# Attention scores and values as 64x64 matmuls on quarters of the array, in a kernel of chunked attention and two expert layers

## The chip, the cores and the metric

The kernel runs on one core of a Trainium2 chip. Its time is the device time of one execution in microseconds; the kernel before takes 1247.1 us (median of three runs, 1245.94 to 1248.13). A core has five engines that work through their own instruction queues and wait for one another with semaphores: PE (TensorE, matmuls out of SBUF into PSUM), DVE (VectorE), ACT (ScalarE), POOL (GpSimd) and SP, which here only issues DMAs. PSUM has eight banks of 128 partitions x 512 f32.

## The reference, cut to what matters

```python
# attention in chunks of 64 tokens; q, k, v are (4, 8, 576, 64)
scores = (q_c @ k_c.T) / sqrt(64)            # 64 x 64 for each batch, head and chunk
scores = scores - max(scores, axis=-1)
attn = exp(scores); attn = attn / (sum(attn) + 1e-9)
x = (attn @ v_c) -> (2304 tokens, 512)
# four relu experts with given shares
out = sum_e p[:, e] * (relu(x @ w1[e]) @ w2[e])    # 512 -> 1024 -> 512
# a gated layer
y = (silu(out @ w_gate) * (out @ w_val)) @ w_out   # 512 -> 1536 -> 512
```

## The kernel before, in words

The 2304 tokens are 18 blocks of 128 tokens. A block holds two chunks of 64 tokens (c = 0, 1) and 8 heads, which lie as 4 pairs (i) of two heads (h). Attention of block a runs in four stages on PE, each followed by work of DVE and ACT:

- **scores** (att_scores, L255): 8 matmuls, one for each pair and chunk. Queries and keys lie with two heads on the 128 partitions (64 each). The keys are laid out with zero blocks (kbd), so that one matmul over 128 rows and 64 columns of the array, with 128 columns streamed, gives both heads. All goes into one PSUM tile of 128 x 512. DVE then takes the maximum (L276) and subtracts it (L277, att_soft), and ACT takes the exponential (L283, att_exp).
- **transposes** (att_turn, L294): four 128x128 transposes through PE into PSUM, a copy of ACT to SBUF (et, L298), and the sums and reciprocals on DVE (att_sums, L302).
- **values** (att_values, L317): 8 matmuls as in the scores, with the values and their zero blocks (vbd); DVE multiplies the result by the reciprocals (L330).
- **output transposes** (att_out, L336): four transposes and a copy of ACT (for blocks 6 to 17: xb, L357), then a DMA.

The zero blocks are written once, by memsets of DVE and POOL at the start (L812), before any matmul of attention.

Blocks 0 to 5 run first (L869 to L918), with the first plain products of the expert layer (plain, L652) behind them. Their stages take PSUM tiles in turn from three pools of two banks each: psA, psX and psY. Blocks 6 to 17 are spread over the expert layer: the list `rest` (L953) holds their 48 stages in order, and they are taken from it one at a time, four in the beginning (`ahead`, L989) and the others in the main loop (L1088):

```python
if rest and now[0] % NPROD < 5:
    stage, a = rest.pop(0)
    stage(a, (psA, "a"))
```

The main loop goes through products: a product (L628) is six matmuls of 128x384 (L624 to L626), and seven products make a set. After four products and after the next three, PE does a piece of the second layer (y, L673 to L677). In the loop a set's products stand as 4, 5 of one set and 0, 1 of the next, y work, 6, then 2, 3, and y work again. Five of the seven are followed by one attention stage: products 6, 2, 3, 4 and 1. Between 6 and 2 and between 2 and 3 only one product stands between two stages; between 3 and 4, 4 and 1, and 1 and 6 there is more.

All stages of blocks 6 to 17 take their PSUM tile from psA, which has two banks, in turn: a stage can start when the stage that had the bank before it has been read out. After each product DVE and ACT do what belongs to it (done, L554), and behind products 6 and 4 DVE also computes two sums of weights (w_sums, L396, `raw<-raw`) before the stage's own work. Engine queues keep the order of the program.

The names in the rows: s, et, av and xt are the PSUM tiles of scores, transposes, values and output transposes; lx, lz, lw and plz, plw, plx the banks of products; hh and hl the hidden values; w the split weights; u and p copies of a product's bank.

Of the kernel before, what the change touches and what calls it, by code (L numbers as in the profile page):

```python
# [19 lines left out]
P = 128  # L20
B, H, S, D = 4, 8, 576, 64
CH = 64
# [69 lines left out]
def attention_moe_gated(  # L92
# [138 lines left out]
    def att_load(a):  # L231
        pool, how = (first_p, dict(tag="q23")) if a in (2, 3) else (at_p, dict(tag="q"))
        q = pool.tile([P, NPAIR, P], F32, name=f"q{a}", bufs=2, **how)
        if a >= 2:
            (nc.scalar if a < 4 else nc.sync).dma_start(q, qt[a])
        for h in range(2):
            b = slice(64 * h, 64 * h + 64)
            queue = nc.scalar if a < 2 and h == 0 else nc.sync
            if a < 2:
                queue.dma_start(flat(q[b]), flat(qt[a, b]))  # L240
            queue.dma_start(flat(kbd[place(a)][b, h]), flat(kt[a, b]))
        att[a] = {"q": q, "k": kbd[place(a)]}

    def att_load_v(a):
        v = vbd[place(a)]
        for h in range(2):
            b = slice(64 * h, 64 * h + 64)
            (nc.scalar if a < 2 and h == 0 else nc.sync).dma_start(flat(v[b, h]), flat(vt[a, b]))
        att[a]["v"] = v
# [4 lines left out]

    def att_scores(a, where):  # L255
        s = att[a]
        ps = att_ps(f"s{a}", where)
        for i in range(NPAIR):
            for c in range(2):
                b = slice(64 * c, 64 * c + 64)  # L260
                nc.tensor.matmul(
                    ps[b, 2 * i : 2 * i + 2], s["q"][:, i, b], s["k"][:, :, i, c], start=True, stop=True
                )
# [6 lines left out]
    def att_soft(a):  # L270
# [3 lines left out]
        pool, how = (acc_p, dict(tag="acc")) if a < BLOCKS else (at_p, dict(tag="e", bufs=3))  # L274
        e = s["e"] = pool.tile([P, H, CH], F32, name=f"e{a}", **how)
        nc.vector.tensor_reduce(out=mx, in_=ps, op=ALU.max, axis=AX.X)  # L276
        nc.vector.tensor_tensor(out=e, in0=ps, in1=mx.unsqueeze(2).to_broadcast(ps.shape), op=ALU.subtract)  # L277
# [16 lines left out]
    def att_turn(a, where):  # L294
        s = att[a]
        ps = transpose(att_ps(f"et{a}", where), s["e"])
        et = s["et"] = at_p.tile([P, H, CH], F32, tag="et", name=f"et{a}", bufs=1)
# [19 lines left out]
    def att_values(a, where):  # L317
        s = att[a]
        ps = att_ps(f"av{a}", where)
        for i in range(NPAIR):  # L320
            for c in range(2):

                nc.tensor.matmul(
                    ps[64 * c : 64 * c + 64, 2 * i : 2 * i + 2],
                    s["et"][:, 2 * i + c, :], s["v"][:, :, i, c], start=True, stop=True,
                )
# [3 lines left out]
        nc.vector.tensor_tensor(  # L330
# [845 lines left out]
```

## Time and profile before

| | |
|---|---|
| three runs, median | 1247.1 us (1245.94 to 1248.13) |
| the profiled execution | 1245.16 us, span 1243.3 us |
| PE busy | 1226.5 us (99%), 7216 matmul records |
| DVE busy | 794.0 us (64%) |
| ACT / POOL busy | 538.7 us (43%) / 595.3 us (48%) |
| DMA | 82.6% of 16 engines, 289 GB/s |

The span is the time from the first to the last instruction of the profiled execution; some 1.9 us lie around it. A matmul with f32 operands shows as two records, one with fp32r operands as one. The busy time of PE counts a matmul's whole passage, so that neighbours overlap; what a matmul costs in a dense stream is the time from its start to the start of the next.

### The profile page before, as it was taken

How to read it: one execution, taken by the hardware profiler on the slowest of the kernel's cores; microseconds unless marked ns; L12 is line 12 of the kernel's file. 1: busy time of each engine (PE TensorE's matmuls, PEld its weight loads, DVE VectorE, ACT ScalarE, POOL GpSimd, SP SyncE). 2: the span in 40 equal slices, each digit the busy share in tenths (PEclk: the TensorE clock that was granted, in tenths of full speed). 3: DMA queues.
4: the chain of work that ended last, by engine and by line, in shares of the span. 5: the costliest groups of instructions: out<-in, count | busy, mean ns of one | idle time of the engine just before them, and what ended most of it. 6: DMA issues, size and time to landing. Idle time of an engine off the chain costs nothing.

```text
span 1243.3 us, 21100 instructions
## 1 busy us (share of the span) xinstructions
PE 1226.5 (99%) x7216; PEld 1131.5 (91%) x7216; DVE 794.0 (64%) x1352; ACT 538.7 (43%) x1192; POOL 595.3 (48%) x611
## 2 busy tenths in 40 slices
PE   7999999999999999999999999999999999999998
PEld 6888888899888999898889889999999999999998
DVE  6766666666636766765566666455667656685576
ACT  4554434345424454544354344334435344344331
POOL 5553434477517776846376867312333222233221
PEclk9999999999999999999999999999999999999999
DMA  9588886799797999897899999866888797788774
GB/s 224 168 273 281 277 271 222 252 323 337 277 354 263 361 325 352 310 380 277 285 368 331 347 395 311 290 226 233 292 322 296 262 312 261 250 312 295 277 234 153
DMA packets 179594, 359.94 MB, mean 289 GB/s; under 512 B 19216, under 2 KB 46352, under 8 KB 179488
## 3 DMA queue, kind: packets, MB, share of 16 engines
q1 hardware_dynamic: 178688, 357.25, 82.6%
q10 hardware_dynamic: 768, 1.31, 0.4%
q8 instruction: 58, 0.95, 0.3%
q14 instruction: 48, 0.39, 0.1%
q0 software_dynamic: 32, 0.04, 0.0%
HBM read 258.90 MB, written 99.61 MB: 288 GB/s over the span
## 4 chain that ended last, share of the span: by engine, by line
PE 81%; DMA 7%; DVE 3%; issue 3%; POOL 2%; ACT 2%; SPq 1%; POOLq 0%; DVEq 0%; ACTq 0%
PE y L673 9%; PE y L677 9%; PE y L675 9%; PE lx L624 8%; PE lx L626 7%; PE lx L625 7%; PE ox L739 5%; PE lz L624 4%; PE oz L739 4%; PE lz L626 4%; PE lz L625 4%; DMA w<-w 3%; PE lw L624 2%; PE lw L626 2%; PE lw L625 2%
## 5 line engine op out<-in xcount | busy, mean ns | idle before, releaser
L673 PE MATMUL y<-w,hh 128*128 128x512 f32 x576 | 228.1, 396 | 0.0
L677 PE MATMUL y<-w,hl 128*128 128x512 f32 x576 | 226.4, 393 | 0.0
L675 PE MATMUL y<-w,hh 128*128 128x512 f32 x576 | 225.6, 392 | 0.2 <-POOL w L126 0.2
L126 POOL TENSOR_TENSOR w<-raw,w 128x256 fp32r<-128x256 f32 (+1 forms) x156 | 143.5, 938 | 149.7 <-ACT w L125 131.9
L126 POOL TENSOR_TENSOR ol<-sg,oh 128x384 fp32r<-128x384 f32 x72 | 80.5, 1129 | 267.1 <-ACT oh L125 225.7
L559 ACT ACTIVATE hh<-sum_p 128x384 fp32r<-128x384 f32 x90 | 47.2, 525 | 221.0 <-DVE sum_p L612 221.0
L762 DVE SCALAR_TENSOR_TENSOR acc<-y,prob,acc 128x512 f32<-128x512 f32 x126 | 91.1, 743 | 65.3 <-PE y L677 65.1
L677 PEld LDWEIGHTS y<-w,hl 128*128 128x128 f32 x576 | 108.0, 188 | 24.1
L673 PEld LDWEIGHTS y<-w,hh 128*128 128x128 f32 x576 | 108.2, 188 | 21.4 <-issue 1.4
L675 PEld LDWEIGHTS y<-w,hh 128*128 128x128 f32 x576 | 108.2, 188 | 21.3 <-POOL w L126 0.7
L612 DVE TENSOR_TENSOR sum_p<-lx,p 128x384 f32<-128x384 f32 x81 | 44.9, 554 | 94.7 <-PE lx L626 93.4
L560 DVE SCALAR_TENSOR_TENSOR hl<-sum_p,hh 128x384 fp32r<-128x384 f32 x90 | 63.0, 700 | 62.4 <-ACT hh L559 62.4
L126 POOL TENSOR_TENSOR w_made<-raw,w_made 128x256 fp32r<-128x256 f32 x84 | 68.3, 822 | 66.3 <-ACT w_made L125 54.3
L125 ACT ACTIVATE w<-raw 128x256 fp32r<-128x256 f32 (+1 forms) x156 | 67.5, 454 | 5.4 <-DVE raw L396 3.2
L125 ACT ACTIVATE oh<-sg 128x384 fp32r<-128x384 f32 x72 | 36.5, 525 | 70.4 <-DVE sg L573 70.0
L608 ACT COPY u<-lx 128x384 f32<-128x384 f32 x81 | 38.6, 477 | 65.0 <-PE lx L626 64.9
L624 PE MATMUL lz<-t1h,w 128*128 128x384 f32 x162 | 55.3, 341 | 1.7 <-DMA w<-w 1.7
L624 PE MATMUL lz<-b22h,w 128*128 128x384 f32 x162 | 55.8, 344 | 1.1 <-ACT p L608 0.9
L624 PE MATMUL lw<-b21h,w 128*128 128x384 f32 x162 | 54.8, 339 | 0.7 <-DMA w<-w 0.7
L125 ACT ACTIVATE o<-sg 128x384 fp32r<-128x384 f32 x54 | 26.5, 520 | 66.8 <-DVE sg L129 66.8
L624 PE MATMUL lx<-t2h,w 128*128 128x384 f32 x162 | 55.0, 340 | 0.3 <-DMA w<-w 0.3
L626 PE MATMUL lx<-t3h,w 128*128 128x384 f32 x162 | 54.9, 339 | 0.0
(270 smaller groups left out, 3421.0 us busy)
## 6 DMA issues: line engine op xcount, KB each, us to landing
w<-w SPq DMA_DIRECT2D x567, 256.0 KB, 5.3
w<-w SPq DMA_DIRECT2D x96, 512.0 KB, 6.0
w<-w_made SPq DMA_DIRECT2D x84, 256.0 KB, 5.7
wo_t<-wo_t SPq DMA_DIRECT2D x36, 512.0 KB, 4.8
wo_b<-wo_b SPq DMA_DIRECT2D x27, 512.0 KB, 4.2
raw<-w SPq DMA_DIRECT2D x19, 512.0 KB, 4.3
raw<-w SPq DMA_DIRECT2D x32, 256.0 KB, 4.3
sums<-x SPq DMA_DIRECT2D x40, 192.0 KB, 5.4
```

The costliest lines, as they stand in the source:

```text
L125: nc.scalar.activation(h, src, AF.Copy)
L126: (lo or nc.vector).tensor_tensor(out=l, in0=src, in1=h.bitcast(F32), op=ALU.subtract)
L559: nc.scalar.activation(h, src, AF.Relu)
L560: nc.vector.scalar_tensor_tensor(out=l, in0=src, scalar=0.0, in1=h.bitcast(F32), op0=ALU.max, op1=ALU.subtract)
L624: nc.tensor.matmul(ps, w[:, 0, c], xh[:, k], start=f, stop=False, skip_group_check=True)
L625: nc.tensor.matmul(ps, w[:, 0, c], xl[:, k], start=False, stop=False, skip_group_check=True)
L626: nc.tensor.matmul(ps, w[:, 1, c], xh[:, k], start=False, stop=e, skip_group_check=True)
L673: nc.tensor.matmul(y, hh[:, c], w[:, 0], start=(j == 0), stop=False)
L675: nc.tensor.matmul(y, hh[:, c], w[:, 1], start=False, stop=False)
L677: nc.tensor.matmul(y, hl[:, c], w[:, 0], start=False, stop=(j == 3))
L739: nc.tensor.matmul(o, left[:, c], w[:, k, right], start=start and t % 2 == 0 and k == 0 and i == 0, stop=k == 1 and i == 2, skip_group_che ...
L762: nc.vector.scalar_tensor_tensor(out=sum_, in0=y, scalar=p, in1=sum_, op0=ALU.mult, op1=ALU.add)
```

## The change

The keys and values lose their zero blocks, and with them the memsets at the start. Each block's scores and values are now 16 matmuls of 64 rows by 64 columns of the array, with 64 columns streamed: one for each pair, head and chunk. The two heads use different rows of the array and write to two PSUM tiles, which lie in two banks, so a stage of scores or values now takes both banks of its pool. DVE reads the two tiles one after the other, with operations of 128x256 in place of 128x512. In blocks 6 to 17 a block's values come two blocks behind the scores and its output transposes three (two before), and the transposes stand ahead of the values. There are two more buffers (et 2, e 4), one DMA for keys and values where there were two (blocks 2 to 17), and one pair of weight splits of the first plain product (w_plain) stands ahead of block 4's softmax.

```diff
@@ -231,36 +231,53 @@
     def att_load(a):
         pool, how = (first_p, dict(tag="q23")) if a in (2, 3) else (at_p, dict(tag="q"))
         q = pool.tile([P, NPAIR, P], F32, name=f"q{a}", bufs=2, **how)
-        if a >= 2:
-            (nc.scalar if a < 4 else nc.sync).dma_start(q, qt[a])
-        for h in range(2):
-            b = slice(64 * h, 64 * h + 64)
-            queue = nc.scalar if a < 2 and h == 0 else nc.sync
-            if a < 2:
+        k = att_tile("k", a)
+        if a < 2:
+            for h in range(2):
+                b = slice(64 * h, 64 * h + 64)
+                queue = nc.scalar if h == 0 else nc.sync
                 queue.dma_start(flat(q[b]), flat(qt[a, b]))
-            queue.dma_start(flat(kbd[place(a)][b, h]), flat(kt[a, b]))
-        att[a] = {"q": q, "k": kbd[place(a)]}
+                queue.dma_start(flat(k[b]), flat(kt[a, b]))
+        else:
+            (nc.scalar if a < 4 else nc.sync).dma_start(flat(q), flat(qt[a]))
+            nc.sync.dma_start(flat(k), flat(kt[a]))
+        att[a] = {"q": q, "k": k}
 
     def att_load_v(a):
-        v = vbd[place(a)]
-        for h in range(2):
-            b = slice(64 * h, 64 * h + 64)
-            (nc.scalar if a < 2 and h == 0 else nc.sync).dma_start(flat(v[b, h]), flat(vt[a, b]))
-        att[a]["v"] = v
+        v = att[a]["v"] = att_tile("v", a)
+        if a < 2:
+            for h in range(2):
+                b = slice(64 * h, 64 * h + 64)
+                (nc.scalar if h == 0 else nc.sync).dma_start(flat(v[b]), flat(vt[a, b]))
+        else:
+            nc.sync.dma_start(flat(v), flat(vt[a]))
+
+    def att_tile(what, a):
+        pool, tag = (first_p, what + "23") if a in (2, 3) else (at_p, what)
+        return pool.tile([P, NPAIR, 2, CH], F32, tag=tag, name=f"{what}{a}", bufs=2)
 
     def att_ps(name, where):
         pool, tag = where
         return pool.tile([P, H, CH], F32, tag=tag, name=name)
 
+    def att_halves(name, where):
+        pool, tag = where
+        return [pool.tile([P, NPAIR, CH], F32, tag=tag, name=f"{name}_{h}") for h in range(2)]
+
+    def by_head(t, h):
+        return t.rearrange("p (i h) k -> p i h k", h=2)[:, :, h]
+
+    def of_head(t, h):
+        return t.rearrange("p (i h) -> p i h", h=2)[:, :, h]
+
     def att_scores(a, where):
         s = att[a]
-        ps = att_ps(f"s{a}", where)
+        ps = att_halves(f"s{a}", where)
         for i in range(NPAIR):
-            for c in range(2):
-                b = slice(64 * c, 64 * c + 64)
-                nc.tensor.matmul(
-                    ps[b, 2 * i : 2 * i + 2], s["q"][:, i, b], s["k"][:, :, i, c], start=True, stop=True
-                )
+            for h in range(2):
+                for c in range(2):
+                    b, r = slice(64 * c, 64 * c + 64), slice(64 * h, 64 * h + 64)
+                    nc.tensor.matmul(ps[h][b, i], s["q"][r, i, b], s["k"][r, i, c], start=True, stop=True)
         if next_in_place(a) is not None:
             att_load(next_in_place(a))
         s["s"] = ps
@@ -271,10 +288,13 @@
         s = att[a]
         ps = s.pop("s")
         mx = st_p.tile([P, H], F32, tag="mx", name=f"mx{a}")
-        pool, how = (acc_p, dict(tag="acc")) if a < BLOCKS else (at_p, dict(tag="e", bufs=3))
+        pool, how = (acc_p, dict(tag="acc")) if a < BLOCKS else (at_p, dict(tag="e", bufs=4))
         e = s["e"] = pool.tile([P, H, CH], F32, name=f"e{a}", **how)
-        nc.vector.tensor_reduce(out=mx, in_=ps, op=ALU.max, axis=AX.X)
-        nc.vector.tensor_tensor(out=e, in0=ps, in1=mx.unsqueeze(2).to_broadcast(ps.shape), op=ALU.subtract)
+        for h in range(2):
+            nc.vector.tensor_reduce(out=of_head(mx, h), in_=ps[h], op=ALU.max, axis=AX.X)
+            nc.vector.tensor_tensor(
+                out=by_head(e, h), in0=ps[h], in1=of_head(mx, h).unsqueeze(2).to_broadcast(ps[h].shape), op=ALU.subtract
+            )
         if a >= BLOCKS:
             att_exp(a)
 
@@ -294,7 +314,7 @@
     def att_turn(a, where):
         s = att[a]
         ps = transpose(att_ps(f"et{a}", where), s["e"])
-        et = s["et"] = at_p.tile([P, H, CH], F32, tag="et", name=f"et{a}", bufs=1)
+        et = s["et"] = at_p.tile([P, H, CH], F32, tag="et", name=f"et{a}", bufs=2)
         nc.scalar.copy(et, ps)
         if a >= BLOCKS:
             att_sums(a)
@@ -316,20 +336,20 @@
 
     def att_values(a, where):
         s = att[a]
-        ps = att_ps(f"av{a}", where)
+        ps = att_halves(f"av{a}", where)
         for i in range(NPAIR):
-            for c in range(2):
-
-                nc.tensor.matmul(
-                    ps[64 * c : 64 * c + 64, 2 * i : 2 * i + 2],
-                    s["et"][:, 2 * i + c, :], s["v"][:, :, i, c], start=True, stop=True,
-                )
+            for h in range(2):
+                for c in range(2):
+                    b, r = slice(64 * c, 64 * c + 64), slice(64 * h, 64 * h + 64)
+                    nc.tensor.matmul(ps[h][b, i], s["et"][r, 2 * i + c], s["v"][r, i, c], start=True, stop=True)
         if next_in_place(a) is not None:
             att_load_v(next_in_place(a))
 
-        nc.vector.tensor_tensor(
-            out=s["e"], in0=ps, in1=s["rs"].unsqueeze(2).to_broadcast(ps.shape), op=ALU.mult
-        )
+        for h in range(2):
+            nc.vector.tensor_tensor(
+                out=by_head(s["e"], h), in0=ps[h],
+                in1=of_head(s["rs"], h).unsqueeze(2).to_broadcast(ps[h].shape), op=ALU.mult,
+            )
 
     x_first = {}
 
@@ -794,31 +814,11 @@
         st_p = at_cm.enter_context(tc.tile_pool(name="st", bufs=3, side="right"))
         first_cm = ExitStack()
         first_p = first_cm.enter_context(tc.tile_pool(name="first", bufs=2))
-        kbd, vbd = [], []
-        for i in range(2):
-            kbd.append(at_p.tile([P, 2, NPAIR, 2, CH], F32, tag=f"k{i}", name=f"kbd{i}", bufs=1))
-            vbd.append(at_p.tile([P, 2, NPAIR, 2, D], F32, tag=f"v{i}", name=f"vbd{i}", bufs=1))
-        for i in range(2):
-            kbd.append(first_p.tile([P, 2, NPAIR, 2, CH], F32, name=f"kbd{2 + i}", bufs=1))
-            vbd.append(first_p.tile([P, 2, NPAIR, 2, D], F32, name=f"vbd{2 + i}", bufs=1))
-
         make_identity(nc, ident)
 
         warm = psY.tile([P, 512], F32, tag="y", name="warm")
         for i in range(WARM):
             nc.tensor.matmul(warm[:, :P], ident, ident, start=True, stop=True)
-        def clear(eng, t):
-            for h in range(2):
-                eng.memset(t[64 * h : 64 * h + 64, 1 - h], 0.0)
-
-        clear(nc.vector, kbd[0])
-        clear(nc.vector, kbd[1])
-        clear(nc.gpsimd, vbd[0])
-        clear(nc.gpsimd, kbd[2])
-        clear(nc.vector, vbd[1])
-        clear(nc.gpsimd, kbd[3])
-        clear(nc.gpsimd, vbd[2])
-        clear(nc.gpsimd, vbd[3])
         nc.gpsimd.dma_start(prob, probs)
         att_load(0)
         att_load(1)
@@ -886,10 +886,10 @@
         att_scores(4, where())
         att_out(2, where())
         att_turn(3, where())
+        w_plain(0, ORDER[:2])
         att_soft(4)
         att_sums(3)
         att_exp(4)
-        w_plain(0, ORDER[:2])
         att_scores(5, where())
         att_soft(5)
         w_plain(0, ORDER[2:])
@@ -951,8 +951,8 @@
         tick()
 
         rest = []
-        for a in range(BLOCKS, NS + 2):
-            for stage, b in ((att_scores, a), (att_values, a - 2), (att_turn, a - 1), (att_out, a - 2)):
+        for a in range(BLOCKS, NS + 3):
+            for stage, b in ((att_scores, a), (att_turn, a - 1), (att_values, a - 2), (att_out, a - 3)):
                 if BLOCKS <= b < NS:
                     rest.append((stage, b))
 
```

Where stages stand changes by one place from block 9 on. In the loop the stages now fall so: scores behind product 6 (blocks 10 and 15), 1 (11 and 16), 4 (12 and 17), 3 (13) and 2 (9 and 14); each is followed by the transposes, the values and the output transposes of earlier blocks at the next three places.

PE's queue around block 10's scores, in the kernel before (six matmuls of a product stand where lines are left out):

```order
L287 MATMUL xt7_1327<-ident_63,e7_948 128x128 x4
...
L261 MATMUL s10_1352<-kbd0_199,q10_1036 64x128 x8
...
L323 MATMUL av8_1385<-vbd0_200,et8_1288 64x128 x8
...
L287 MATMUL et9_1439<-ident_63,e9_1182 128x128 x4
```

and in the changed kernel:

```order
L307 MATMUL xt6_1457<-ident_63,e6_1024 128x128 x4
...
L280 MATMUL s10_0_1497<-k10_1174,q10_1173 64x64 x2
L280 MATMUL s10_1_1498<-k10_1174,q10_1173 64x64 x2
...
L307 MATMUL et9_1543<-ident_63,e9_1315 128x128 x4
...
L344 MATMUL av8_0_1570<-v8_1252,et8_1343 64x64 x2
L344 MATMUL av8_1_1571<-v8_1252,et8_1343 64x64 x2
```

The scores come one place earlier, behind product 6, and their next neighbour is et9, which needs the bank of s10_0; before it was av8, with a bank that xt7 had used.

DVE's queue at the same place, before:

```order
L560 SCALAR_TENSOR_TENSOR hl_1_3_0_1317<-lx_3_1046,hh_1_3_0_1316 128x384
L396 TENSOR_TENSOR raw1_5_1141<-raw1_5_1141 128x256 x2
L276 TENSOR_REDUCE mx10_1365<-s10_1352 128x8
L277 TENSOR_TENSOR e10_1366<-s10_1352,mx10_1365 128x512
L330 TENSOR_TENSOR e8_1041<-av8_1385,rs8_1293 128x512
```

and now:

```order
L580 SCALAR_TENSOR_TENSOR hl_1_3_0_1487<-lx_3_1185,hh_1_3_0_1486 128x384
L416 TENSOR_TENSOR raw1_5_1290<-raw1_5_1290 128x256 x2
L294 TENSOR_REDUCE mx10_1519<-s10_0_1497 128x4
L295 TENSOR_TENSOR e10_1520<-s10_0_1497,mx10_1519 128x4x64
L294 TENSOR_REDUCE mx10_1519<-s10_1_1498 128x4
L295 TENSOR_TENSOR e10_1520<-s10_1_1498,mx10_1519 128x4x64
L332 TENSOR_REDUCE sm9_1550<-e9_1315 128x8
```

The sums of weights stand ahead of the softmax in both; the softmax itself is now four operations.

ACT's queue from block 10's exponential to the copy of et9, now:

```order
L303 ACTIVATE e10_1520<-e10_1520 128x512
L628 COPY u_4_1532<-lx_4_1425 128x384
L125 ACTIVATE w2_1_3_1534<-raw2_1_3_1332 128x512
L125 ACTIVATE w_4_3_1538<-raw1_4_820 128x256
L318 COPY et9_1548<-et9_1543 128x512
```

Before, et8's copy stood seven entries ahead of this exponential, and et9's six behind it.

## Rows read from the trace of the kernel before

**Rows 1.** Windows: length, then busy PE, PEld, DVE, ACT, POOL; clock, DMA, GB/s.
```profile
10.00:24.00 14.00, 10.79 (x140) 9.11 (x140) 10.26 (x23) 7.59 (x18) 6.34 (x10) 1.00 1.01 241
52.00:235.00 183.00, 183.00 (x1198) 158.16 (x1197) 119.82 (x202) 79.98 (x190) 81.17 (x91) 1.00 0.76 254
```
**Rows 2.** Timeline of PE: start, length, what, count; a values stage between products.
```profile
161.05 0.34 PE L625 MATMUL lx<-t3l,w 128*128 128x384 f32 x1
161.23 0.34 PE L626 MATMUL lx<-t3h,w 128*128 128x384 f32 x1
161.50 1.09 PE L323 MATMUL av<-vbd,et 128*64 128x128 f32 x16
...
162.80 0.33 PE L625 MATMUL lz<-b22l,w 128*128 128x384 f32 x1
```
**Rows 3.** By source line: shortest, median, longest record in ns.
```profile
L323 PE MATMUL av<-vbd,et x288: 272/273/323, 11.5 to 232.7; 128*64 128x128 f32 x144
```
**Rows 4.** Timeline of PE, the first records of the program.
```profile
1.38 3.79 PE L809 MATMUL warm<-ident 128*128 128x128 f32 x16 [1.38 <-POOL ident masks.py:199]
5.98 3.68 PE L261 MATMUL s<-kbd,q 128*64 128x128 f32 x32 [0.82 <-DMA kbd<-kt]
```
**Rows 5.** Timeline of DVE: half-sized and whole operations on a PSUM tile.
```profile
21.53 0.42 DVE L129 TENSOR_TENSOR b11l<-xt,b11h 128x256 fp32r<-128x256 f32 x1 [1.44 <-ACT b21h L346]
95.05 0.69 DVE L276 TENSOR_REDUCE mx<-s 128x8 f32<-128x512 f32 x1
```
**Rows 6.** Timeline, behind product 6: PE's stage, DVE's sums of weights at two places.
```profile
111.76 1.09 PE L261 MATMUL s<-kbd,q 128*64 128x128 f32 x16
112.86 1.35 DVE L396 TENSOR_TENSOR raw<-raw 128x256 f32<-128x256 f32 x2
...
94.07 0.87 DVE L396 TENSOR_TENSOR raw<-raw 128x256 f32<-128x256 f32 x2
```
**Rows 7.** Timeline of ACT: an exponential, what follows, a copy of et; two splits.
```profile
115.57 0.63 ACT L283 ACTIVATE e<-e 128x512 f32<-128x512 f32 x1 [2.91 <-DVE e L277]
116.11 0.46 ACT L608 COPY u<-lx 128x384 f32<-128x384 f32 x1
116.47 0.42 ACT L125 ACTIVATE w<-raw 128x256 fp32r<-128x256 f32 x1
...
117.46 0.59 ACT L298 COPY et<-et 128x512 f32<-128x512 f32 x1
...
94.44 0.94 ACT L125 ACTIVATE w<-raw 128x512 fp32r<-128x512 f32 x2
```
**Rows 8.** Timeline, values behind product 6: PE, DVE, and the next two stages.
```profile
131.92 1.09 PE L323 MATMUL av<-vbd,et 128*64 128x128 f32 x16
133.02 1.85 DVE L396 TENSOR_TENSOR raw<-raw 128x256 f32<-128x256 f32 x2
134.11 0.60 PE L287 MATMUL et<-ident,e 128*128 128x128 f32 x4
134.79 0.68 DVE L330 TENSOR_TENSOR e<-av,rs 128x512 f32<-128x512 f32 x1
135.60 0.60 PE L287 MATMUL xt<-ident,e 128*128 128x128 f32 x4
```
**Rows 9.** Timeline, behind product 4, and the next stage.
```profile
121.84 0.60 PE L287 MATMUL xt<-ident,e 128*128 128x128 f32 x4
123.74 1.85 DVE L396 TENSOR_TENSOR raw<-raw 128x256 f32<-128x256 f32 x2
...
125.51 0.88 PE L261 MATMUL s<-kbd,q 128*64 128x128 f32 x12
```
**Rows 10.** Timeline of the start: one period of blocks 0 to 3, the first plain product.
```profile
13.40 0.66 PE L287 MATMUL et<-ident,e 128*128 128x128 f32 x4
...
16.69 0.66 PE L287 MATMUL et<-ident,e 128*128 128x128 f32 x4
...
24.63 0.44 PE L624 MATMUL plz<-b11h,w 128*128 128x384 f32 x1 [1.91 <-ACT w L125]
```

## The prediction

> **What bounds the kernel now.** I read first the windows of the two stretches in which attention runs. From 52 to 235 us, where blocks 6 to 17 lie in the expert layer, PE is busy in all 183.00 us, while DVE has 119.82, ACT 79.98 and POOL 81.17; the view of waits of this stretch has no line of PE. From 10 to 24 us, blocks 0 to 3, PE is busy 10.79 of 14.00 us and DVE 10.26 [rows 1]. So in the loop a shorter stage of PE is worth its full length and a new wait of PE costs its full length; in the start only what lies on the chain counts.
>
> Then I read what a stage costs there. Between the last record of one product (161.23) and the second of the next (162.80) lie 1.57 us where two plain steps of 0.18 (161.05 to 161.23) would do: 1.21 us for a stage [rows 2]. Its 16 records take 1.09 from the first start to the last end, one takes 0.27 [rows 2, 3]: (1.09 - 0.27) / 15 = 0.055 from start to start, 0.875 for 16. The other 0.33 goes into entering and leaving the stage, and stays.
>
> **PE's matmuls.** The change makes 16 records of 128 columns into 32 of 64. How many quarters of the array work at once, no row shows. The first records of the program bound it: 16 records on the whole array take 3.79 us (0.237 each), 32 records of the same 128 columns on half of its columns 3.68 (0.115 each) [rows 4]. So two halves do work at once now, each record twice as long as the 0.055 says. A record of 64 columns then takes 0.055 in its quarter. Four at once: 32 x 0.055 / 4 = 0.44 a stage, 0.44 less than now. Two at once: 0.875, no change. One at a time: 1.75, 0.875 more. Less than 0.44 is excluded, since there are four quarters. I take four: halves in columns are seen to overlap, and the halves in rows have partitions and banks of their own. 24 stages in the loop: -10.6 us.
>
> The rows show no mean step of small records under 0.055 us [rows 3], and 0.44 / 32 = 0.014 is wanted. The Trainium skill (TensorE: Matmul & The Clock Gate, section "Back-to-back issue gap") says against this that from start to start no matmul takes less than about 25 ns; by that rule the stage takes 32 x 0.025 = 0.80 and saves 0.07, which is near rival 1. The same page ("Part 3: Packing small matmuls") gives some 4 ns between matmuls on different tiles, by which the 0.44 stands. The trace of before cannot tell the two apart.
>
> **The banks.** A stage of scores or values now holds both banks of psA, so every stage must wait for the stage just before it to be read, where before it had a whole stage between. Priced for the loop, with one PSUM operation of DVE on half a tile at 0.42 us where the whole takes 0.69 [rows 5]; the two halves of a softmax take four, 0.15 x 2 more than now, beside PE's work unless named below.
>
> *Scores behind product 6 (blocks 10, 15).* DVE has the sums of weights first: they end 112.86 + 1.35 - 111.76 = 2.45 us after the stage's start [rows 6]. Reduction and subtraction of the first half, with handovers, end at 3.4, of the second at 4.3. The transposes take the first half's bank. They are due one product later: from one stage of values to the next stage it is now 134.11 - 131.92 = 2.19 [rows 8], less 0.44: 1.75. Wait 1.65, twice. Next the values, due 135.60 - 134.11 = 1.49 behind the transposes [rows 8], at 4.9. Their second bank is that of the transposes, which ACT copies only after the block's exponential (from 4.3), a copy of u and one split of weights (block 15) or two (block 10). By the starts 115.57, 116.11 and 116.47, the copy's 0.59 and 0.94 for two splits [rows 7], et is copied at 6.1 or 6.65. Wait 1.2 and 1.75. Together 6.25.
>
> *Values behind product 6 (blocks 10, 15, 17).* The product with the reciprocals starts at 134.79 in DVE's queue, behind 1.85 us of sums; its first half would end 0.47 later, 3.35 after 131.92 [rows 8]. The output transposes are due at 1.75: wait 1.6, twice, and 1.0 for block 17, where no other softmax loads DVE. Together 4.2. Before, the output transposes came two places later, at 135.60, just behind the 135.47 at which DVE was done [rows 8].
>
> *Scores behind product 4 (blocks 12, 17).* Sums end at 123.74 + 1.85 - 121.84 = 3.75, the first half is read at 4.7. Due: 125.51 - 121.84 = 3.67 [rows 9], with the stage's 0.77 in place of the transposes' 0.51 (1.49 less a product of 0.98): 3.93. Wait 0.75, twice: 1.5.
>
> *The other places.* Some twelve more pairs of neighbours (blocks 6 to 9 in front, values behind product 2, scores behind product 2) come out by the same reckoning between 0 and 0.9, mostly under 0.3; I take 3.4 in all and bound it by 0 and 8.
>
> Waits in the loop: 6.25 + 4.2 + 1.5 + 3.4 = 15.4 us. Nothing gives them back: PE has no other idle time there to absorb them [rows 1], and what is queued behind the waiting matmul is PE's own products, for which everybody else waits.
>
> **The start.** The memsets hide behind the first loads and idle engines: nothing. The first two blocks' scores take half of 3.68 [rows 4]; block 0's softmax starts earlier, but DVE needs 0.3 longer for it: -0.4. A period of blocks 0 to 3 takes 16.69 - 13.40 = 3.29 [rows 10]; DVE gets three times 0.15 us more work in it and was busy 73% of the stretch, and values wait for both halves of a softmax now. I take +0.26 for three periods, +0.8 (bounds: the saved PE time of 0.88 a period fully gained, -2.6; or 0.6 lost, +1.8). The first plain product waits 1.91 for ACT's split of weights [rows 10], which now stands ahead of an exponential of 0.63 [rows 7]: -0.6. The values of blocks 3 to 5 lie between dense products: 3 x 0.44 = -1.3. Together -1.5 (bounds -5 and +3). The fewer DMAs and further buffers: nothing, since no wait of PE in the loop is for them.
>
> **Sum.** 15.4 - 10.6 - 1.5 = +3.3 us on the profiled execution's 1245.16: 1248.5. The median of the runs shown is 1.9 above that execution, so I forecast 1250 for the changed kernel.
>
> **The rivals.**
> 1. *The matmuls gain nothing.* Two quarters at once, 0.875 a stage as now. Some 13 waits follow a stage of scores or values; that stage being 0.44 longer, they shrink by as much, to 9.7 in all. The start comes out at +0.2: +9.9 us, 1257. For it: no row shows steps under 0.055. Against: the overlap of halves. By the Trainium skill's 25 ns (the page above) the loop would gain 1.7 us more than that.
> 2. *Faster: DVE clears in time.* The place is the sums of weights ahead of a softmax or a product with the reciprocals; the price of a pair is 0.87 us at 94.07, against 1.35 and 1.85 elsewhere [rows 6, 8, 9]. With 0.87 everywhere the waits are 5.3 behind product 6's scores, 1.7 behind its values, none behind product 4 and 1.5 elsewhere: 8.5, and 8.5 - 10.6 - 1.5 = -3.6: 1243.5. It decides from 12.1 us of waits down. Against: three of the four pairs shown take the longer time, and nothing in the change makes them shorter.
> 3. *One quarter at a time.* 24 x 0.875 = 21, waits about 6, the start +2: +29, 1276. Against: the halves.
> 4. *The clock.* The start has less work of PE between its waits; if the granted clock stayed at 1.2 GHz to 24 us, PE's part of that chain would double, some +5: 1255. The rows show 1.00 from 10 us on [rows 1].
>
> **How the numbers follow.** Forecast 0.45 (its own range 1246 to 1255), rival 1 0.18, rival 2 0.25, rival 3 0.05, rival 4 0.07. No change that a measurement can tell is 0.2%, 2.5 us: 1244.6 to 1249.6. Faster: most of rival 2 and a corner of the forecast, 0.25. Same: 0.17. Slower: 0.58. The range reaches from rival 2 with a better start, 1242, to rival 1 with its full waits, 1259.
>
> **What would show it.** In the loop a stage of scores should take 0.7 us from the first start to the last end, not 1.09 (rival 1: 1.1; rival 3: over 1.7). PE should show waits for DVE's subtraction and multiplication and for ACT's copies of et, in sum some 15 us between 52 and 235, the longest behind product 6; under 12 the forecast's sign is wrong. The time after 235 us should be the same length as before. I am wrong, too, if the start moves by more than 4 us.

## The result and the profile after

The changed kernel takes 1253.62 us (median of six runs, 1252.09 to 1258.39), the kernel before, beside it, 1246.74 us (six runs). The ratio is 1.0059, with a 95% interval of 1.0041 to 1.0076: slower by 6.9 us, where the forecast of 1250 meant 2.9. The time lies within the forecast's own range of 1246 to 1255. The profiled execution's span went from 1243.3 to 1251.5 us.

To see where the 8.2 us arise, I set the same matmul of both traces side by side. The product records of the changed kernel start 1.03 us later at the first plain product, 1.97 us at 45 us, 7.56 at 240 and 8.12 at 1222. So the start loses 2.0 us, the loop in which blocks 6 to 17 lie 5.6, and the rest 0.6.

**The loop.** The windows of the changed kernel, to be held against [rows 1] (window, length, then busy PE, PEld, DVE, ACT, POOL, the clock, DMA):

```profile
10.00:24.00 14.00, 10.13 (x222) 8.50 (x220) 9.36 (x29) 7.26 (x17) 5.60 (x9) 1.00 0.83 294
52.00:240.00 188.00, 176.55 (x1576) 150.40 (x1575) 124.38 (x242) 80.96 (x190) 81.32 (x90) 1.00 0.72 249
```

PE, which had no idle time here, now has 11.45 us of it in 188. The view of waits of PE, empty for the kernel before, names three causes between 52 and 245 us (total, times, longest):

```profile
PE xt L307 <- DVE e L349: 4.6, 5, 1.4
PE et L307 <- DVE e L295: 4.5, 4, 1.9
PE av L344 <- ACT et L318: 2.2, 3, 1.1
```

These are the three waits that the prediction priced: output transposes for the product with the reciprocals, transposes for the softmax, values for the copy of the transposed weights. The timeline shows one chain of them, block 10 behind products 6 and 2 (start, length, engine, line, what; idle time ahead in brackets). It answers to [rows 2, 6, 7]:

```profile
92.94 0.34 PE L646 MATMUL lx<-t4h,w 128*128 128x384 f32 x1
93.21 0.69 PE L280 MATMUL s<-k,q 64*64 64x64 f32 x32
93.83 0.45 PE L644 MATMUL lx<-t2h,w 128*128 128x384 f32 x1
...
94.81 0.34 PE L646 MATMUL lx<-t2h,w 128*128 128x384 f32 x1
96.61 0.63 PE L307 MATMUL et<-ident,e 128*128 128x128 f32 x4 [1.45 <-DVE e L295]
...
98.22 0.33 PE L344 MATMUL av<-v,et 64*64 64x64 f32 x4
99.64 0.57 PE L344 MATMUL av<-v,et 64*64 64x64 f32 x23 [1.10 <-ACT et L318]
...
94.31 1.35 DVE L416 TENSOR_TENSOR raw<-raw 128x256 f32<-128x256 f32 x2
95.58 0.42 DVE L294 TENSOR_REDUCE mx<-s 128x4 f32<-128x256 f32 x1
96.03 0.42 DVE L295 TENSOR_TENSOR e<-s,mx 128x256 f32<-128x256 f32 x1
96.38 0.41 DVE L294 TENSOR_REDUCE mx<-s 128x4 f32<-128x256 f32 x1
96.83 0.42 DVE L295 TENSOR_TENSOR e<-s,mx 128x256 f32<-128x256 f32 x1
...
97.28 0.63 ACT L303 ACTIVATE e<-e 128x512 f32<-128x512 f32 x1 [3.17 <-DVE e L295]
97.82 0.46 ACT L628 COPY u<-lx 128x384 f32<-128x384 f32 x1
98.18 0.93 ACT L125 ACTIVATE w<-raw 128x512 fp32r<-128x512 f32 x2
99.02 0.57 ACT L318 COPY et<-et 128x512 f32<-128x512 f32 x1
```

A stage of 32 small records takes 0.69 us where 16 wide ones took 1.09 [rows 2]. The scores are done at 93.90, but DVE first has the sums of weights (94.31), and the first half is free only when the first L295 ends at 96.45; the transposes follow at 96.61, 1.80 behind the record before them instead of 0.18. The values then find their second bank held until ACT's copy of et ends at 99.59, behind an exponential, a copy of u and two splits.

Wait by wait, from such rows (a start less the usual 0.18 or 0.27 behind the record before it, and what a stage is longer than 0.69): scores behind product 6, 1.61 and 2.09 for the transposes, 1.42 and 0.89 for the values; values behind product 6, 1.54, 1.54 and 1.07; scores behind product 4, 0.73 twice; the other places 2.9, of it 0.6 twice at values behind product 2 and 0.9 at a stage of values at 73 us. Together 14.5 us. (The view of waits names 11.3 of them, since it counts PE as busy to the end of the last record's passage.)

**The start.** PE, against [rows 10], with the windows around the fall of the clock:

```profile
13.00 1.11 PE L307 MATMUL et<-ident,e 128*128 128x128 f32 x4
13.91 1.06 PE L307 MATMUL xt<-ident,e 128*128 128x128 f32 x4
...
17.73 0.66 PE L307 MATMUL et<-ident,e 128*128 128x128 f32 x4
...
21.23 0.60 PE L307 MATMUL et<-ident,e 128*128 128x128 f32 x4
23.77 0.33 PE L280 MATMUL s<-k,q 64*64 64x64 f32 x4 [1.94 <-issue]
24.61 1.12 PE L280 MATMUL s<-k,q 64*64 64x64 f32 x28 [0.50 <-DVE e L295]
25.66 0.69 PE L644 MATMUL plz<-b11h,w 128*128 128x384 f32 x1
```

```profile
17.30:24.10 6.80, 4.03 (x87) 3.25 (x86) 4.64 (x15) 4.00 (x10) 2.89 (x5) 1.00 0.59 193
24.10:30.90 6.80, 6.30 (x74) 5.66 (x73) 3.84 (x9) 2.76 (x7) 2.79 (x4) 0.50 0.50 157
30.90:52.00 21.10, 20.48 (x180) 18.95 (x177) 17.17 (x37) 12.95 (x34) 12.03 (x15) 1.00 0.42 140
```

Two things are new. PE stands still for 1.94 us ahead of block 5's scores: they need both banks of psX, and block 4's scores lie there until DVE has read them. The first plain product stands behind them in PE's queue. And the granted clock is 0.50 (1.2 GHz) from 24.1 to 30.9 us, behind PE's idle time from 21.8 to 23.8. Earlier, too, PE ran at the lower level for longer: the transposes take 1.06 to 1.11 us at 13.0 and 13.9 where those of before take 0.66 at 13.40 [rows 10], and 0.60 to 0.66 only from 17.7 on. (The windows show 1.00 there, but the trace has no record of the clock before 17.3 us; the durations tell. The trace of e5 below has the record: 0.50 from 9.65 to 16.48 us, and transposes of 1.11 and 1.06 in it.)

### The profile page after: what moved, and what is told of

It is laid out like the page before. It is cut to its first block, busy times and chain, and to the rows that moved or that the text cites. A ratio compares the mean times of both kernels' runs of the same rounds, so it can differ in the third digit from the quotient of the medians.

```text
span 1251.5 us, 22235 instructions
## 1 busy us (share of the span) xinstructions
PE 1222.3 (98%) x7792; PEld 1125.7 (90%) x7792; DVE 795.6 (64%) x1400; ACT 539.3 (43%) x1192; POOL 589.3 (47%) x601
## 4 chain that ended last, share of the span: by engine, by line
PE 75%; DMA 6%; issue 5%; DVE 5%; POOL 4%; SPq 3%; ACT 2%; ACTq 0%; POOLq 0%; DVEq 0%
PE y L693 8%; PE y L697 8%; PE y L695 8%; PE lx L644 7%; PE lx L646 7%; PE lx L645 7%; PE ox L759 5%; PE oz L759 4%; PE lz L644 4%; PE lz L646 3%; PE lz L645 3%; DMA w<-w 3%; PE lw L644 2%; PE lw L646 2%; PE lw L645 2%
```

## The experiments

All were timed against the kernel before on the same chip, so ratios compare one experiment with another better than times do. Each has one trace. Where a place is given in a trace, it is how much later the same product record starts than in the trace of before.

**1. The quarters in the old order (e2_lag_two).** The lag of three and the transposes ahead of the values are undone.

```diff
-        for a in range(BLOCKS, NS + 3):
-            for stage, b in ((att_scores, a), (att_turn, a - 1), (att_values, a - 2), (att_out, a - 3)):
+        for a in range(BLOCKS, NS + 2):
+            for stage, b in ((att_scores, a), (att_values, a - 2), (att_turn, a - 1), (att_out, a - 2)):
```

> Edit: the changed kernel with the stages of blocks 6 to 17 in the order of before (scores, values and transposes, output transposes with lag two). My theory: the loss in the loop comes from the two banks that a stage of scores or values now holds, so that each stage waits for its neighbour, whatever the order: about 12 us of waits between 52 and 245 us against 14.5 now, and a time of 1250 to 1254 us. Rival: the new order with lag three makes the waits; then they go, and the time falls to about 1241 to 1243.

Measured: 1255.71 us, ratio 1.0079 (1.0066 to 1.0092). That is 1.7 us over the expected range; the mean granted clock of its runs is 0.994, of the changed kernel's 0.996. Its waits between 59 and 241 us add up to 13.9 us, about as many as with the new order. So the order of the stages is not where the time went.

**2. The stage ahead of the sums of weights (e3_stage_first, and e4_before_stage_first as control).** In the main loop the call that issues splits and sums of weights goes behind the attention stage, in the changed kernel (e3) and in the kernel before (e4).

```diff
-            if now[0] + LEAD < len(prods):
-                prepare(*prods[now[0] + LEAD])
...
             if rest and now[0] % NPROD < 5:
                 stage, a = rest.pop(0)
                 stage(a, (psA, "a"))
+            if now[0] + LEAD < len(prods):
+                prepare(*prods[now[0] + LEAD])
```

> Edit: the changed kernel, but in the main loop a stage is issued ahead of what the loop prepares for later products (sums of weights on DVE, splits on ACT and POOL) instead of behind it. PE's order is the same. My theory: PE waits for DVE and ACT, which have this preparation ahead of the reading of the banks; with it behind, the waits fall from 14.5 to about 4 us and the time to about 1243. Rival: the waits come from the stages' own work on DVE and ACT (four operations, the exponential, the copy); then they stay above 10 us and the time stays within 3 us of 1253.

> The same edit in the kernel before, as a control: PE has no waits in the loop there, so nothing can go; 1245 to 1249 us. If it is faster by more than 3 us, the edit does something else than take waits away.

Measured: e3 1245.20 us, ratio 0.9993 (0.9982 to 1.0004), 2 us above the expected 1243; e4 1246.38 us, 1.0003 (0.9994 to 1.0011). The same block 10 in e3, PE, then DVE, then the window of the loop:

```profile
91.62 0.69 PE L280 MATMUL s<-k,q 64*64 64x64 f32 x32
...
93.74 0.63 PE L307 MATMUL et<-ident,e 128*128 128x128 f32 x4 [0.18 <-DVE e L295]
...
92.72 0.41 DVE L294 TENSOR_REDUCE mx<-s 128x4 f32<-128x256 f32 x1
93.17 0.42 DVE L295 TENSOR_TENSOR e<-s,mx 128x256 f32<-128x256 f32 x1
...
94.30 0.88 DVE L416 TENSOR_TENSOR raw<-raw 128x256 f32<-128x256 f32 x2
```

```profile
52.00:240.00 188.00, 184.24 (x1627) 159.40 (x1626) 122.59 (x244) 83.66 (x194) 82.73 (x94) 1.00 0.75 258
```

DVE reads the scores 1.10 us after they start, not 2.37, and the wait of 1.45 is one of 0.18. PE's idle time in the loop is 3.76 us in place of 11.45, and the loop goes from +5.6 to -3.8 us. Counted as above, 5.5 of the 14.5 us of waits are left; 2.9 of them are values that wait for ACT's copy of et, and the two longest of these (1.41 and 0.90) are as long as before the edit. The order alone is worth nothing to the kernel before, which had no such waits. This shows both halves of the loop's sum: small stages gain, waits for the read-out take it back.

**3. Two banks without quarters (e10_two_banks_only, e11_two_banks_stage_first).** The kernel before, with its wide matmuls and its order; only the scores and values of blocks 6 to 17 go to two tiles in two banks, by pairs, and DVE reads them in halves. e11 has the stage first as well.

```diff
+    def att_banks(name, where, a):
+        n = NPAIR if a < BLOCKS else NPAIR // 2
+        pool, tag = where
+        return [pool.tile([P, 2 * n, CH], F32, tag=tag, name=f"{name}_{g}") for g in range(NPAIR // n)], n
...
-                    ps[b, 2 * i : 2 * i + 2], s["q"][:, i, b], s["k"][:, :, i, c], start=True, stop=True
+                    ps[i // n][b, 2 * (i % n) : 2 * (i % n) + 2], s["q"][:, i, b], s["k"][:, :, i, c], start=True, stop=True
```

> The kernel before, full-width matmuls with zero blocks and its order of stages, but the scores and values of blocks 6 to 17 are written to two tiles in two banks (pairs 0 and 1, pairs 2 and 3), which DVE reads one after the other in halves of 128x256, as the changed kernel does. This takes the second part of the change alone, in the loop alone. My theory: the waits for the two banks are what the loop of the changed kernel loses, whatever the matmuls; with quarters and the same order of stages the waits between 59 and 241 us add up to some 15 us, so this kernel takes 1246 + 15 = 1261 us (1259 to 1263), ratio 1.010 to 1.014. The rival: the waits belong to the quarter matmuls (their dispatch, or their halves that finish together), and two banks alone cost no more than DVE's two additional operations a stage, 0.15 us at most where PE waits for them: 1246 to 1248 us, ratio 1.000 to 1.002.

> The run before with the stage issued ahead of the splits and sums of weights in the main loop. My theory: DVE then reads the banks out ahead of the sums of weights, and of the 15 us of waits some 4 to 5 stay, as with quarters (3.7 us in the rows of the run with the stage first): 1246 + 5 = 1251 us (1249 to 1252), ratio 1.003 to 1.005. The rival: what the order gained with quarters came from elsewhere than the read-out of the banks, and this run is as the one before it: 1259 us or more.

Measured: e10 1252.83 us, ratio 1.0055 (1.0041 to 1.0069); e11 1247.67 us, 1.0002 (0.9993 to 1.0012). Both expectations for e10 missed. Its waits add up to 6.9 us, half of those with quarters, and its products stand 6.98 us later at 240 us: two banks alone cost 7 us. e11 is faster than the 1249 to 1252 that were expected: the view of waits names only 0.2 us, and the loop loses 1.2. The stage of values that follows the scores behind product 6, in e10 (PE and DVE):

```profile
112.39 1.09 PE L266 MATMUL s<-kbd,q 128*64 128x128 f32 x16
...
115.74 0.66 PE L333 MATMUL av<-vbd,et 128*64 128x128 f32 x8 [1.00 <-PE lx L638]
116.57 0.66 PE L333 MATMUL av<-vbd,et 128*64 128x128 f32 x8 [0.18 <-DVE e L285]
117.16 0.44 PE L636 MATMUL lz<-t1h,w 128*128 128x384 f32 x1
...
116.43 0.42 DVE L342 TENSOR_TENSOR e<-av,rs 128x256 f32<-128x256 f32 x1
```

and the same stage with quarters in the same order (e2_lag_two):

```profile
113.47 0.69 PE L280 MATMUL s<-k,q 64*64 64x64 f32 x32
...
116.83 0.33 PE L344 MATMUL av<-v,et 64*64 64x64 f32 x4 [1.41 <-issue]
117.66 0.68 PE L344 MATMUL av<-v,et 64*64 64x64 f32 x28 [0.50 <-DVE e L295]
118.28 0.44 PE L644 MATMUL lz<-t1h,w 128*128 128x384 f32 x1
...
118.30 0.76 DVE L349 TENSOR_TENSOR e<-av,rs 128x256 f32<-128x256 f32 x2 [0.78 <-PE av L344]
```

In e10 half the stage runs while the second bank is still held, and DVE reads the first bank (116.43) before the second half has started. With quarters only 4 of the 32 records get through before the second bank is needed, and both banks are complete only at the end.

**4. Quarters head by head (e13_head_by_head).** This run asks whether the alternation of heads makes the longer waits: e2 with the loops turned, so that head 0 fills its bank first.

```diff
-        for i in range(NPAIR):
-            for h in range(2):
+        for h in range(2):
+            for i in range(NPAIR):
                 for c in range(2):
```

> The quarters with the stages in the order of before (ratio 1.0079, waits of some 15 us between 59 and 241 us), but each stage issues its 16 matmuls head by head: all of head 0 of the pairs into the one bank, then all of head 1 into the other. In the run with two banks alone the waits were 6.9 us, not 15, and there the first bank was complete when half the stage was done, and the second first needed then. My theory now: half of the waits come from heads that alternate, so that both banks are needed at the stage's start and are complete only at its end; head by head the waits fall to 6 to 8 us, while at most two quarters can work at once, so that a stage takes 1.0 to 1.1 us again in place of 0.69 and the 24 stages lose some 9 us. Together 1255 to 1258 us, ratio 1.007 to 1.010. The rival: the waits of 15 us belong to the quarters as such (more records, two banks from different rows of the array); then they stay and the longer stages add 9 us: 1264 us, ratio 1.014 to 1.016.

Measured: 1255.35 us, ratio 1.0070 (1.0055 to 1.0084). The time is in the expected range. With two quarters in use at a time, not four, the stage takes 0.97 us. The same place as above:

```profile
114.36 0.97 PE L280 MATMUL s<-k,q 64*64 64x64 f32 x32
...
117.72 0.68 PE L344 MATMUL av<-v,et 64*64 64x64 f32 x16 [1.11 <-issue]
118.55 0.68 PE L344 MATMUL av<-v,et 64*64 64x64 f32 x16 [0.15 <-DVE e L295]
119.16 0.44 PE L644 MATMUL lz<-t1h,w 128*128 128x384 f32 x1
```

and in the kernel before, where block 10's scores start at 111.76 [rows 6]:

```profile
115.06 0.44 PE L624 MATMUL lz<-t1h,w 128*128 128x384 f32 x1
```

Its waits are 8.9 us, not 13.9 (6 to 8 expected, 15 for the rival). But they are counted over a stage of 0.97 and not of 0.69, and the rows above show that this is nearly the whole difference. From the start of the scores to the product behind the next values it takes 4.81 us with heads that alternate (113.47 to 118.28), 4.80 head by head (114.36 to 119.16) and 4.77 with wide matmuls in two banks (112.39 to 117.16), against 3.30 in the kernel before (111.76 to 115.06). The read-out sets the end of the wait: DVE starts on the scores 2.37 to 2.38 us after they start in all three, behind the sums of weights. A stage that is shorter by 0.3 or 0.4 only waits longer by as much. The same holds, within 0.05 us, wherever these three kernels wait for both banks but at one place, the values at 97.44 us in e2 (3.88 from scores to product there, 3.59 head by head, 3.41 in e10).

So the theory above, that half of the waits come from heads that alternate, is not shown. Of the 9.6 us that 24 shorter stages save in e2, 7.0 turn into longer waits (13.9 against e10's 6.9), and 2.6 remain: e2's loop stands at +4.5 and e10's at +7.0. Head by head is no better than e2: 8.9 of waits less 24 x 0.12 of shorter stages is 6.0, and 6.15 is what the trace shows.

**5. The start's parts (e5_scores5_bank, e6_split_late).** e5 gives block 5's scores the banks of psY; e6 puts the first pair of weight splits back behind block 4's exponential.

```diff
-        att_scores(5, where())
+        where()
+        att_scores(5, (psY, "y"))
```

```diff
-        w_plain(0, ORDER[:2])
         att_soft(4)
         att_sums(3)
         att_exp(4)
+        w_plain(0, ORDER[:2])
```

> Edit: the changed kernel with block 5's scores in psY instead of psX. My theory of the start: those scores stand 1.9 us at the two banks that block 4's scores hold until their softmax is done, and the first plain product waits behind them; with another pool they start at 23.5 instead of 23.8 and run through, and end near 24.4 instead of 25.7: 1.0 to 1.3 us faster, and up to 2.5 if PE's clock then stays at its higher level. Rival: the first plain product waits for the split weights anyway; then no change within 0.5 us.

> The changed kernel with one edit of it undone: the first pair of weight splits of the first plain product stands behind block 4's exponential again. My theory: block 5's scores, which wait for block 4's softmax to read both banks of psX, hold the first plain product, not the splits, so the move gained nothing: 1253 to 1254.5 us, ratio to the kernel before 1.005 to 1.0065, and the first plain product still starts behind block 5's scores, at 25 to 26 us of the profile. The rival, as the prediction had it: the move is worth 0.6 us, so this kernel takes 1254.2 us or more and the first plain product starts later than 25.66 by 0.6.

Measured: e5 1251.99 us, ratio 1.0054 (1.0042 to 1.0066), less than expected and not told from the changed kernel's 1.0059 by the intervals; in its trace the first plain product starts at 24.54, not 25.66. In that trace the fall of the clock behind the wait is gone as well: the granted clock is 1.00 from 16.48 to 176.90 us, and at 45 us the products stand 0.37 us earlier than before, not 1.97 later. e6 takes 1254.03 us, 1.0070 (1.0058 to 1.0083), with the first plain product at 25.64: the move of the splits gained nothing there. Its time is in the expected range, its ratio just above it. The upper part of e6's interval leaves room for the rival's 0.6 us; the product's place does not.

**6. PE's idle time filled (e7_fill_idle, e8_fill_early).** Matmuls of the identity, whose result is not used, where PE stood idle in the start: e7 has 8 ahead of block 5's scores, e8 two more ahead of block 0's transposes and two behind them.

```diff
+        fill = psL.tile([P, 512], F32, tag="w", name="fill")
+        for i in range(FILL):
+            nc.tensor.matmul(fill[:, :P], ident, ident, start=True, stop=True)
         w_plain(0, ORDER[:2])
         att_soft(4)
```

> The changed kernel with 8 more matmuls of the identity (16 records of 128x128, some 1.7 us at 2.4 GHz) ahead of block 5's scores, where PE stands idle for 1.94 us (21.83 to 23.77) in the changed kernel's profile; their result is not used. My theory: the granted clock falls to 1.2 GHz at 24.1 us because PE stood idle before; with the gap filled it stays at 2.4 GHz through 24 to 31 us, the mean clock of the runs comes up by some 0.002, the products of that stretch keep a spacing of 0.17 us, and the time is some 1.2 us below the changed kernel's: 1252.4 us, ratio 1.0045 to 1.0050. The rival: the clock falls because matmuls on quarters of the array are what runs there; then it falls all the same and the time is that of the changed kernel or up to 0.3 us more, ratio 1.0059 to 1.0062.

> The filler of the run before, and 2 more such matmuls ahead of block 0's transposes and 2 behind them, where PE stands idle for 0.68 us each (8.53 and 10.31 us). In the changed kernel's profile the clock comes up to 2.4 GHz at 17.3 us (10.0 in the kernel before), and block 0's and 1's transposes run at half rate. My theory: the idle places keep it down; with them filled it comes up by 14 us at the latest, which is worth up to 1.4 us more than the filler at block 5 alone: 1251.0 us, ratio 1.0035 to 1.0045. The rival (the quarter matmuls themselves keep it down): it comes up at 17 us as before and the time is that of the filler at block 5 alone or 0.3 us more.

Measured: e7 1253.48 us, ratio 1.0063 (1.0044 to 1.0082); e8 1251.00 us, 1.0036 (1.0023 to 1.0049), as expected. In e7's trace the clock stays at 2.4 GHz through the stretch in which it fell, and at 45 us the products stand 0.15 us earlier than before, not 1.97 later. But the time did not follow. The six runs spread from 1250.7 to 1258.0 us, and the interval holds what either expectation said. In the profiled execution (1256.87 us) the clock fell in the loop instead.

```profile
17.60:178.00 160.40, 150.35 (x1445) 130.07 (x1444) 114.43 (x230) 75.16 (x179) 74.86 (x87) 1.00 0.70 240
178.00:184.80 6.80, 6.50 (x45) 4.92 (x44) 0.96 (x4) 1.73 (x5) 1.45 (x2) 0.50 0.52 186
```

Ahead of it, at 176.57, the transposes of block 15 had waited 1.93 us for DVE, the longest of the waits. e5's trace has a fall behind the same wait (176.9 to 180.3 us), the changed kernel's own has none there. With the early filler (e8) PE is at 2.4 GHz from 14.4 us on and stays there, and at 45 us the products stand 0.61 us earlier than before. That it doesn't take quarters to lower the clock is shown by e4, with wide matmuls: PE idle for 2.37 us, then a fall in the plain products.

```profile
24.20 0.44 PE L624 MATMUL plz<-b11h,w 128*128 128x384 f32 x1 [2.37 <-ACT w L125]
```

```profile
25.40:28.80 3.40, 3.40 (x16) 2.96 (x16) 0.10 (x1) 1.08 (x2) 1.63 (x3) 0.50 0.84 216
```

Up to the first plain product e4, e10 and e11 are the kernel before, in which the gap was 1.91 us and no fall followed. In all three the gap is 2.37 us. In e11 the clock fell as in e4 (25.63 to 29.04 us); in e10 it did not:

```profile
25.40:28.80 3.40, 3.39 (x31) 2.97 (x31) 1.31 (x3) 1.18 (x3) 2.04 (x3) 1.00 0.95 214
```

So whether the clock falls there differs from one execution to the next. At 45 us e4's products stand 1.09 us later than before and e11's 0.89, e10's 0.06 earlier. A start that is compared by one trace of each kernel carries about 1 us of this.

**7. All together (e9_stage_first_fill, e12_stage_first_fill_all).** e3, e5 and 6 filler matmuls ahead of block 5's scores; e12 with the early filler too. The diffs are those above.

> The changed kernel with three edits: in the main loop the attention stage is issued ahead of the splits and sums of weights (as in the run with the stage first, ratio 0.9993), block 5's scores take the other pool's banks, and 6 matmuls of the identity fill PE's idle time ahead of them. My theory: the gains add, 0.6 us for the bank and about 0.9 us for the clock, since in the run with the stage first it fell for 3.4 us: 1243.7 us, ratio 0.9975 to 0.9985, below the kernel before. The rival (the clock's falls come from elsewhere in the loop, and the start's gains are hidden): 1245 us, ratio 0.999 to 1.000.

> The best kernel so far (stage first, block 5's scores in the other pool's banks, filler ahead of them: ratio 0.9976) with the early filler as well: 2 matmuls of the identity ahead of block 0's transposes and 2 behind. My theory: the clock comes up earlier in the start by some us, which was worth 0.45 us in the products' places when it was added to the filler at block 5 alone: 1242.5 us, ratio 0.9968 to 0.9976. The rival: the other filler already holds the clock from 15 us on and the early one only costs PE time: 1243 to 1243.5 us, ratio 0.9976 to 0.9982.

Measured: e9 1242.94 us, ratio 0.9976 (0.9967 to 0.9985), as expected; e12 1242.48 us, 0.9961 (0.9949 to 0.9974), the expected time at a slightly lower ratio. Both are faster than either kernel; which of the two is better the intervals don't tell. In e12's trace the loop stands at -3.9 us against before, and its mean granted clock is 0.999 over five runs, like that of before, where the changed kernel has 0.996.

## Why the prediction came out as it did

- **The matmuls, -10.6 us.** Right in kind: four quarters work at once. A stage went from 1.09 to 0.69, 0.40 less and not 0.44: 24 x 0.40 = 9.6. With it rivals 1 and 3 fall. From record to record that is (0.69 - 0.27) / 31 = 0.014 us, from matmul to matmul (two records each) 0.42 / 15 = 0.028. The Trainium skill gives a start-to-start floor of some 25 ns ("TensorE: Matmul & The Clock Gate", section "Back-to-back issue gap"). The prediction set that floor on each of the 32 records; so set, the trace does not agree with it (0.014), while per matmul the mean of 0.028 lies just above it.
- **The waits, +15.4 us.** 14.5 in the rows, each place within 0.5: 1.65 was forecast twice for the transposes (1.61, 2.09), 1.75 and 1.2 for the values (1.42, 0.89), 1.6, 1.6 and 1.0 (1.54, 1.54, 1.07), 0.75 twice (0.73, 0.73), 3.4 for the rest (2.9). The loop's sum was to be +4.8. By the rows it is 14.5 - 9.6 = +4.9, in which two misses of about 1 us cancel; that is luck. The trace has +5.6: behind each wait of transposes the next product starts 0.03 to 0.06 us later than usual. Experiment 2 shows that 9.0 of the 14.5 us come from what stands ahead of the read-out, by its rows DVE's sums of weights. Experiments 3 and 4 show that a wait ends at the same moment whether the stage is long or short, so that about half of the waits is time which the quarters had saved. The prediction reckons so in rival 1, where stages longer by 0.44 shrink the waits to 9.7.
- **The start, -1.5 us.** This is the term that failed: it is +2.0 in the trace. The first scores came as forecast, -0.4 at 13 us. From there to block 2's transposes it lost 1.44 us where the working had 0.26 for a period; in this stretch PE was at 1.2 GHz until 17 us. The -0.6 for the moved splits is 0, because the product behind them stands behind block 5's scores, which wait for both banks of psX; the prediction priced such waits in the loop and in the periods of blocks 0 to 3, and none for block 5. And the -1.3 of blocks 3 to 5 was eaten by the fall from 24.1 to 30.9 us. With the idle time filled the products at 45 us stand at -0.15 (e7) and -0.61 (e8). So filling the idle time gives back 2.1 to 2.6 of the 3.5 us. These are not a part beside the wait for psX: e5, which takes away the wait alone, stands at -0.37 there, and its clock did not fall behind block 4. The wait and the clock behind it are one chain, and how much of it a single execution shows is in part chance (experiment 6).
- **The rivals.** Rival 4 had the right mechanism, the clock, for another stretch (to 24 us). It was given 0.07, and its price stood beside the start's term instead of in its bounds. Rival 2, DVE in time, is what experiment 2 makes true: there the kernel comes out 8.4 us faster than as changed, level with the kernel before.

The start's miss (3.5 us) and the loop's (0.8) add up to 4.3 of profile, and 1248.5 was worked out for an execution that took 1254.32; the other 1.5 us lie behind 240 us (0.6) and around the span (2.8 us against 1.9), and their cause is not known.

## What to carry to other kernels

When a stage takes all banks of its pool, look up for every stage what its reader has in the queue ahead of the read-out, and move that behind it: here this was worth 8.4 us to the changed kernel and nothing to the one before. Where a read-out sets the end of a wait, a shorter stage ahead of it gains nothing: of the 9.6 us that the 24 shorter stages saved in e2, 7.0 became longer waits. A new wait of about 2 us on PE should be priced twice, once as idle time and once as the clock that may fall behind it.

## What the runs showed of the hardware

32 records of 64x64 on four quarters, which alternate, take 0.69 us, on two quarters at a time 0.97, and 16 wide ones 1.09. The granted clock fell to 0.50 behind idle times of PE of 1.94 us (24.1 to 30.9), 1.93 us (e7, e5) and 2.37 us (e4), and not each time: the same 1.93 us at 178.70 in the changed kernel's trace, 1.91 us in the kernel before [rows 10] and 2.37 us in e10 were followed by none. What else decides it stays open.
